# Eight shared PSUM banks and three PV blocks a unit in an attention and GLU kernel on one core

## The chip, the cores and the metric

One Trainium2 chip, one of its cores. The metric is the time of one execution on the device in microseconds (us); lower is better. The kernel before has a median of 1634.21 us over three executions (1633.94 to 1635.79).

## The reference, cut to what matters

The input x has 2048 rows of 512 numbers. The result mixes two branches by a gate for each row:

```
g = sigmoid((x * gate_w).sum(-1))
q = x @ wq          # 32 heads of 16 numbers
k = x @ wk; v = x @ wv      # one head, shared by all 32
p = softmax(q . k * 16 ** -0.5)
a = (p @ v, heads side by side) @ wo
h = (x @ w_gate) * (x @ w_up)       # 512 -> 1792
b = h @ w_down
out = g * a + (1 - g) * b
```

Nearly all of the work is in three places: the scores (32 heads of 2048 x 2048 with a depth of only 16), their exponentials, and the bilinear GLU branch.

## The kernel before, in words

The attention is cut into 64 units. A unit is a chunk of 512 rows of x (c), a group of eight heads (g) and a quarter of the chunk (t, 128 queries). For each unit three kinds of work stand on TensorE:

- **s1** (`p1`, matmul L690): the scores with the queries on the partitions, 32 matmuls of 512 columns. VectorE takes the largest score of each row out of the PSUM bank (L691). The negative maximum goes through DRAM back into two rows of the unit's Q tile.
- **s2** (`p2`, matmul L731): the scores again with the keys on the partitions, the maximum already taken off, 32 matmuls of 512 columns. ScalarE writes the exponentials from the bank into a tile P (L732).
- **PV** (`pv`, matmul L744): P times V. A round takes two key blocks: four matmuls in the program's order, on four column groups of 32, and eight in the trace, which shows each of these matmuls twice. A unit has eight rounds, all summed in one PSUM bank, the accumulator. After the last round ScalarE copies it out (L748), and a chain of DMAs and GpSimd operations (`o_chain`) brings it to the output projection.

Everything else of any size (the query projections, the GLU matmuls, the output projection) is cut into jobs of twelve products. Each product is run as two matmuls of 64 rows, one in each half of the array. They are the **filler** (`fill`, L854, tiles called ms). s1, s2 and filler matmuls use one half of the array's rows each, so that two run side by side; the kernel calls the halves lanes 0 and 1. PV uses all the rows.

TensorE's order is written out by hand. `ORDER` (L51) is a string of 144 letters that is run through once a unit: a and b are s1 on lane 0 and 1, c and d are s2, e and f filler, p a PV round. A run of p's without another letter between is called a **block** here, and what lies between two passes of the same letter a **cycle**; each other letter is a **slot**. Ahead of the first pass a loop runs s1 and filler alone until 25 s1 matmuls of each lane are done (`LEAD`).

A tile of PSUM fills one of eight banks, and a bank is named when the program is built. While it writes the order out, the Python code keeps a clock for each engine (`State`, L394): when each bank would come free, when TensorE could go on. `claim` (L417) gives an s1, s2 or filler matmul the bank that would be free soonest. The chip knows nothing of these clocks: there, a matmul that begins in a bank waits on a semaphore for the engine that read the bank's last tenant, wherever the planner's clock thought it was. Before the change seven banks (`NB = 7`) are in this pool, and bank 7 is the accumulator's alone (`pv`, L737 on).

The two lanes of a filler job sum into one bank. Where lane 1 would begin a job whose products of lane 0 are not yet known to be through, `fill` first calls `fence` (L811): two small transposes with a copy by VectorE between them, for which TensorE has to wait once.

The chunk of x that the filler works on changes three times. Those places are called turns in what follows; they fall into the 18th, the 33rd and the 48th unit's stretch or right behind.

Of the kernel before, what the change touches and what calls it, by code (L numbers as in the profile page):

```python
# [32 lines left out]
PBUF = 12  # L33
# [5 lines left out]
GAP = 50.0  # L39
# [2 lines left out]
EXP, EXP_END = 482.0, 604.0  # L42
COPY, COPY_END = 497.0, 597.0
PV_IN, PV_ROUND, PV_LAST, PV_END, PV_OUT = 331.0, 866.0, 438.0, 617.0, 647.0
NB = 7
LAT, LAT_LAST = 1.0, 0.5
LEADJOBS = 6
O0, O1 = 0, 0


ORDER = (  # L51
    "cbebedefcfefcbefedebefcfafedefadefcfebefefebededafefedafefedafcfefcbefef"
    "cfcfafadppdafcaffafcfcfefafefcbedebefedefafedebebedebappcdcbabppadcbabpp"
)
HALVES = (slice(0, 64), slice(64, 128))
KROWS = (slice(0, 48), slice(64, 112))
# [4 lines left out]
def mix_kernel(ctx: ExitStack, tc: tile.TileContext, x, wq, wk, wv, wo, wg, wu, wd, gw, out):  # L61
# [87 lines left out]
    def bank(i, name):  # L149
        return psum.tile([128, 512], F32, name=name, tag=f"bank{i}")  # L150
# [25 lines left out]
    st = {"gen": None, "next": None, "q": 0, "tail": False, "idle": False}  # L176
# [217 lines left out]
    class State:  # L394


        def __init__(self):
            self.nl, self.last, self.pd = [0.0, 0.0], -1e9, 0.0
            self.dve, self.act = 4000.0, 500.0
            self.free, self.wrote = [0.0] * NB, [0] * NB  # L400
            self.known, self.seq = 0, 0
            self.n1, self.n2, self.npv = [0, 0], [0, 0], 0
            self.ready, self.slot, self.acc = {}, [[0.0, 0.0] for _ in range(PBUF)], 0.0
            self.inpv = False

        def issue(self, l, wait):
# [10 lines left out]
        def claim(self):  # L417
            b = self.free.index(min(self.free))
            if st["idle"] or self.npv == 0:
                b = max((i for i in range(NB) if self.free[i] <= max(min(self.nl), self.free[b])), key=lambda i: self.wrote[i])  # L420
            self.known = max(self.known, self.wrote[b])
# [21 lines left out]
        def pv(self):  # L443
            s = self.npv
            at = self.last + PV_ROUND - PV_LAST if self.inpv else max(self.last + PV_IN, self.pd)
            for i in range(2):
                for v in range(2):
                    t, seq = self.ready.pop((s + i, v))
                    at, self.known = max(at, t), max(self.known, seq)
            if s % NJ == 0:  # L450
                at = max(at, self.acc)
            for i in range(2):
                self.slot[(s + i) % PBUF] = [at + PV_LAST + PV_END] * 2
            self.last = self.pd = at + PV_LAST
            self.inpv = True
            self.nl = [self.last + PV_OUT] * 2
            self.seq += 1
            self.npv += 2
            if self.npv % NJ == 0:
                self.act = max(self.act, self.last + PV_END) + COPY  # L460
                self.acc = self.act + COPY_END - COPY + GAP

    def evac(j, p, part):
        clock["act"] = max(clock["act"], clock["T"] + SEEN)
# [113 lines left out]
    def o_chain(c, g, t, osb):  # L578
        if (c, t) not in oT:
            oT[c, t] = work.tile([128, 4, 128], F32, name="oT", bufs=2)  # L580
        dst = oT[c, t][:, g]
        d = dram.tile([128, 512], F32, name="do", tag="do", bufs=4)
        dn = work.tile([128, 2, 8], F32, name="dn", bufs=2)
        raw = work.tile([128, 2, 128], F32, name="raw", bufs=2)
        rb = work.tile([128, 128], F32, name="rb", bufs=2)
        d4 = d.rearrange("(p a r) (s q) -> p a r s q", p=2, a=2, s=4)

        m = LAT if units.index((c, g, t)) < NU - 2 else LAT_LAST

        def store():  # L590
            nc.sync.dma_start(d, osb)
            later(5500.0 * m, load)

        def load():
            for par in range(2):
                nc.sync.dma_start(dn[:, par], d[par * 64 + 16:par * 64 + 64:32, :].rearrange("a (m e) -> a m e", e=8))
            for par in range(2):
                for half in range(2):
                    nc.sync.dma_start(raw[half * 64:half * 64 + 64, par],
                                      d4[par, half, 0:DH].rearrange("r s q -> s r q"))  # L600
            later(6000.0 * m, add)

        def add():
            den = work.tile([128, 8], F32, name="den", bufs=2)
            nc.gpsimd.tensor_tensor(den, dn[:, 0], dn[:, 1], op=OP.add)
            end = spend("pool", 200.0)
            nc.gpsimd.tensor_tensor(raw[:, 0], raw[:, 0], raw[:, 1], op=OP.add)
            spend("pool", 400.0)
            at(end + 2500.0 * m, lambda: recip(den))

        def recip(den):
            rc = work.tile([128, 8], F32, name="rc", bufs=2)
            nc.vector.reciprocal(rc, den)
            at(spend("dve", 150.0) + 250.0, lambda: rows(rc))

        def rows(rc):
            dr = dram.tile([8, 128], F32, name="dr", tag="dr", bufs=4)
            nc.sync.dma_start(dr.rearrange("h (m e) -> (h m) e", e=8), rc)
            later(3000.0 * m, lambda: spread(dr))

        def spread(dr):
            nc.sync.dma_start(rb, dr.rearrange("h (o q) -> h o q", o=1).to_broadcast([8, DH, 128]))
            later(3500.0 * m, norm)

        def norm():
            nc.gpsimd.tensor_tensor(dst, raw[:, 0], rb, op=OP.mult)  # L626
            spend("pool", 400.0)
            if (c, g, t) == units[NU - 2]:
                oh, ol = st["o"] = w512("oh", F32R, 2), w512("ol", F32R, 2)
                o = oT[c, t].rearrange("p g q -> p (g q)")[:, 0:384]  # L630
                done = split2(oh[:, 0:384], ol[:, 0:384], o) + 300.0
                st["p"] = bank(6, "wo")
                front.append(Job(
                    lambda: [m for k in range(3)
                             for m in mm3((oh[:, KS[k]], ol[:, KS[k]]), (woh[:, k], wol[:, k]))],
                    None, lambda: done if st["tail"] else 1e18, st["p"]))
            elif g == NG - 1:
                o = oT.pop((c, t)).rearrange("p g q -> p (g q)")
                oh, ol = w512("oh", F32R, 2), w512("ol", F32R, 2)
                done = split2(oh, ol, o) + 300.0  # L640
                front.append(Job(
                    lambda: [m for k in range(4)
                             for m in mm3((oh[:, KS[k]], ol[:, KS[k]]), (woh[:, k], wol[:, k]))],
                    lambda p, i: y_add(c, t, p, gg[:, c * NT + t:c * NT + t + 1]), lambda: done))
        at(E.acc + 50.0, store)
# [11 lines left out]

    def o_last(c, g, t, osb):
        def pick():
            p = bank(5, "pick")  # L660
            for v in (1, 0):
                for s in range(4):
                    nc.tensor.matmul(p[:, v * 128:v * 128 + 128], st["sel"][v][:, s], osb[:, KS[s]],  # L663
                                     start=(s == 0), stop=(s == 3))
            rb = work.tile([128, 128], F32, name="rb", bufs=2)
            nc.vector.reciprocal(rb, p[:, 128:256])
            o = oT[c, t][:, g]
            nc.vector.tensor_tensor(o, p[:, 0:128], rb, op=OP.mult)
            oh, ol = st["o"]
            split(oh[:, KS[3]], ol[:, KS[3]], o)  # L670
            front.append(Job(lambda: mm3((oh[:, KS[3]], ol[:, KS[3]]), (woh[:, 3], wol[:, 3])),
                             lambda p, i, at=clock["T"] + 2500.0: y_add(c, t, p, gg[:, c * NT + t:c * NT + t + 1]),
                             lambda at=clock["T"] + 2500.0: at, st["p"], False))
        later(900.0, pick)
# [59 lines left out]
    acc = {}  # L734

    def pv(s):
        u, j = divmod(s, NJ)  # L737
        if j == 0:
            acc[u] = bank(7, "acc")
        for i in range(2):  # L740
            src = P.pop(s + i)
            for half in range(2):
                b = 32 * (2 * i + half)
                nc.tensor.matmul(acc[u][b:b + 32, :], V[:, j + i], src[:, half], start=(j == 0), stop=(j == NJ - 2))  # L744
        if j == NJ - 2:
            def out():
                osb = w512("osb", F32, 2)
                nc.scalar.copy(osb, acc.pop(u))  # L748
                (o_last if u == NU - 1 else o_chain)(*units[u], osb)
            later(0.0, out)  # L750


    p = bank(6, "warm")
# [6 lines left out]
    p = ms_bank(1)  # L760
# [37 lines left out]
    st["gen"] = ffn_jobs()  # L798
    E = State()
    E.n1, E.dve, E.act = [done, done], 2000.0, 2000.0  # L800
    E.free = [2500.0, 3500.0, 0.0] + [1500.0] * (NB - 3)
    fetched = 2
    jobs = {}

# [140 lines left out]
    while events or front or st["gen"] or st["next"]:  # L945
        run_events()
        if peek():
# [3 lines left out]
            for part in range(j.parts):  # L951
                p = j.p
                if p is None:
                    p = ms_bank(turn)
# [24 lines left out]
```

## Time and profile before

| what | value |
| --- | --- |
| median of three executions | 1634.21 us |
| span of the profiled execution | 1631.8 us |
| what lies around the span, median less span | 2.4 us |
| granted TensorE clock | 1.000 |
| TensorE matmuls busy | 1622.0 us (99%) |
| VectorE busy | 1386.9 us (85%) |
| ScalarE busy | 1239.0 us (76%) |
| GpSimd busy | 719.4 us (44%) |

PE is TensorE, DVE is VectorE, ACT is ScalarE and POOL is GpSimd. Matmuls of the two lanes overlap and their ends are modelled, so that the 99% doesn't say that nothing is lost: what counts is when one matmul starts after the one before. A row of the timeline gives the start, the time from the start of the first to the end of the last, the engine, the line, out<-in, and how many instructions are merged (x16). In brackets stands the idle time ahead of it and who ended it. L12 is line 12 of the kernel.

### The profile page before, as it was taken

How to read it: one execution, taken by the hardware profiler on the slowest of the kernel's cores; microseconds unless marked ns; L12 is line 12 of the kernel's file. 1: busy time of each engine (PE TensorE's matmuls, PEld its weight loads, DVE VectorE, ACT ScalarE, POOL GpSimd, SP SyncE). 2: the span in 40 equal slices, each digit the busy share in tenths (PEclk: the TensorE clock that was granted, in tenths of full speed). 3: DMA queues.
4: the chain of work that ended last, by engine and by line, in shares of the span. 5: the costliest groups of instructions: out<-in, count | busy, mean ns of one | idle time of the engine just before them, and what ended most of it. 6: DMA issues, size and time to landing. Idle time of an engine off the chain costs nothing.

```text
span 1631.8 us, 35270 instructions
## 1 busy us (share of the span) xinstructions
PE 1622.0 (99%) x13126; PEld 1047.5 (64%) x13126; DVE 1386.9 (85%) x2415; ACT 1239.0 (76%) x2395; POOL 719.4 (44%) x855
## 2 busy tenths in 40 slices
PE   9999999999999999999999999999999999999999
PEld 7666666666675666666665666666665676676665
DVE  6988888888887888888887888888888888898871
ACT  4787777787786787787786777787787787787785
POOL 5515642724532652625422651643724641642621
PEclk9999999999999999999999999999999999999999
DMA  5463322212122221212122221222223221222101
GB/s 160 163 220 117 91 67 59 60 52 75 51 86 83 77 68 55 63 54 68 56 90 74 74 65 54 66 59 61 58 54 117 65 78 50 62 66 58 35 27 38
DMA packets 184991, 121.44 MB, mean 74 GB/s; under 512 B 46196, under 2 KB 154356, under 8 KB 184820
## 3 DMA queue, kind: packets, MB, share of 16 engines
q1 hardware_dynamic: 183620, 118.87, 24.3%
q8 instruction: 103, 1.69, 0.4%
q14 instruction: 68, 0.56, 0.1%
q10 hardware_dynamic: 1200, 0.33, 0.1%
HBM read 82.96 MB, written 36.17 MB: 73 GB/s over the span
## 4 chain that ended last, share of the span: by engine, by line
PE 96%; DVE 2%; issue 1%; DMA 1%; ACT 0%; POOL 0%; SPq 0%; POOLq 0%; ACTq 0%; DVEq 0%
PE ms L854 33%; PE acc L744 29%; PE s L731 18%; PE s L690 14%; DVE mx L691 2%; PE ms L142 1%; ACT P L732 0%; DMA dq<-oh 0%; PE warm L755 0%; PE wo L142 0%; DMA rb<-dr 0%; DMA dr<-rc 0%; SPq L218 0%; PE pick L663 0%; DMA Q<-dq 0%
## 5 line engine op out<-in xcount | busy, mean ns | idle before, releaser
L691 DVE TENSOR_REDUCE mx<-s 128x1 f32<-128x512 f32 x2048 | 1309.6, 684 | 180.4 <-PE s L690 103.3
L732 ACT ACTIVATE P<-s 128x512 f32<-128x512 f32 x2048 | 1079.1, 604 | 272.1 <-PE s L731 201.0
L731 PE MATMUL s<-Q,KK 50*128 50x512 f32 x2048 | 747.7, 412 | 0.3
L690 PE MATMUL s<-KK,Q 48*128 48x512 f32 x2048 | 691.6, 407 | 1.9 <-ACT P L732 1.0
L744 PE MATMUL acc<-P,V 128*32 128x512 f32 x4096 | 492.5, 598 | 0.0
L731 PEld LDWEIGHTS s<-Q,KK 50*128 50x128 f32 x2048 | 351.8, 185 | 188.1 <-issue 99.8
L690 PEld LDWEIGHTS s<-KK,Q 48*128 48x128 f32 x2048 | 338.7, 185 | 99.4 <-ACT P L732 55.4
L854 PE MATMUL ms<-xh,wh 64*128 64x512 f32 x920 | 338.9, 392 | 0.0
L854 PE MATMUL ms<-xl,wh 64*128 64x512 f32 x920 | 336.6, 391 | 0.0
L854 PE MATMUL ms<-xh,wl 64*128 64x512 f32 x920 | 321.4, 392 | 0.0
L744 PEld LDWEIGHTS acc<-P,V 128*32 128x32 f32 x4096 | 108.9, 109 | 234.8 <-issue 197.2
L527 POOL TENSOR_TENSOR hf<-gs 128x512 f32<-128x512 f32 x55 | 70.6, 1284 | 361.5 <-ACT gs L518 314.5
L356 POOL TENSOR_TENSOR y<-y,yt 128x512 f32<-128x512 f32 x63 | 81.0, 1286 | 234.3 <-ACT yt L355 223.9
L854 PEld LDWEIGHTS ms<-xh,wh 64*128 64x128 f32 x920 | 163.5, 185 | 9.9 <-DVE mx L691 0.4
L854 PEld LDWEIGHTS ms<-xl,wh 64*128 64x128 f32 x920 | 164.8, 186 | 7.7
L854 PE MATMUL ms<-wdh,hh 64*128 64x512 f32 x448 | 168.0, 394 | 0.1
L854 PE MATMUL ms<-wdl,hh 64*128 64x512 f32 x448 | 167.2, 393 | 0.6 <-POOL wdl L130 0.6
L854 PEld LDWEIGHTS ms<-xh,wl 64*128 64x128 f32 x920 | 157.2, 186 | 9.5 <-issue 0.3
L854 PE MATMUL ms<-wdh,hl 64*128 64x512 f32 x448 | 160.0, 393 | 0.0
L130 POOL TENSOR_TENSOR wl<-wn,wh 128x512 fp32r<-128x512 f32 x116 | 149.5, 1289 | 9.3
L626 POOL TENSOR_TENSOR oT<-raw,rb 128x128 f32<-128x128 f32 x63 | 29.1, 463 | 163.0 <-DMA rb<-dr 163.0
L748 ACT COPY osb<-acc 128x512 f32<-128x512 f32 x64 | 37.6, 587 | 78.6 <-PE acc L744 78.6
(154 smaller groups left out, 1331.3 us busy)
## 6 DMA issues: line engine op xcount, KB each, us to landing
do<-osb SPq DMA_DIRECT2D x63, 256.0 KB
wn<-in_B_w_gate_dram SPq DMA_DIRECT2D x56, 256.0 KB
wn<-in_B_w_up_dram SPq DMA_DIRECT2D x56, 256.0 KB
wdn<-in_B_w_down_dram SPq DMA_DIRECT2D x56, 256.0 KB
Q<-dq SPq DMA_DIRECT2D x384, 32.0 KB
raw<-do SPq DMA_DIRECT2D x252, 32.0 KB
dq<-oh SPq DMA_DIRECT2D x16, 256.0 KB
dq<-ol SPq DMA_DIRECT2D x16, 256.0 KB
```

Of the source, the lines that this page charges most:

```text
L130: nc.gpsimd.tensor_tensor(lo, src, hi.bitcast(F32), op=OP.subtract)
L142: nc.tensor.matmul(p, l, r, start=start and i == 0, stop=stop and i == len(prods) - 1)
L356: nc.gpsimd.tensor_tensor(y[c, t], y[c, t], tmp, op=OP.add)
L527: nc.gpsimd.tensor_tensor(hf, gu[0], gu[1], op=OP.mult)
L626: nc.gpsimd.tensor_tensor(dst, raw[:, 0], rb, op=OP.mult)
L690: nc.tensor.matmul(p, q[r, slot], KK[r, kq * 512:(kq + 1) * 512], start=True, stop=True)
L691: nc.vector.tensor_reduce(mx[u][:, half * 4 + slot, kq:kq + 1], p, axis=AX.X, op=OP.max)
L731: nc.tensor.matmul(p, KK[r, j * 128:(j + 1) * 128], q[r].rearrange("p s q -> p (s q)"), start=True, stop=True)
L732: nc.scalar.activation(P[s][:, half], p, AF.Exp, scale=0.25)
L744: nc.tensor.matmul(acc[u][b:b + 32, :], V[:, j + i], src[:, half], start=(j == 0), stop=(j == NJ - 2))
L748: nc.scalar.copy(osb, acc.pop(u))
L854: nc.tensor.matmul(j.p[part], lhs[HALVES[l]], rhs[HALVES[l]], start=(l == 0 and i == 0), stop=(l == 1 and end))
```

## The change

All eight banks are in the planner's pool (`NB = 8`). The accumulator has no bank of its own: at a unit's first round `pv` claims one, keeps it until the last round, and gives it back once ScalarE has copied it. `ORDER` is another string. It has the same letters (16 each of a, b, c and d, 36 each of e and f, eight p), but the eight rounds stand in three blocks (3, 2 and 3 rounds) and not in four (2, 2, 2, 2). Two banks that were named by number in the last steps (the last output projection, and the `pick` matmuls that sort out the last unit's result) give way if the accumulator holds them. The order of the instructions differs, and with it the banks; what is computed does not.

```
-NB = 7
+NB = 8
...
-    "cbebedefcfefcbefedebefcfafedefadefcfebefefebededafedafefedafcfefcbefef"
...
+    "adcbcfefefebedebedbedefcfebebcfefcfefafcfaefebededefbedebededefadeafeffc"
...
             if s % NJ == 0:
-                at = max(at, self.acc)
+                self.accb = self.claim()
+                at = max(at, self.free[self.accb])
+                self.free[self.accb] = 1e18
...
             if self.npv % NJ == 0:
                 self.act = max(self.act, self.last + PV_END) + COPY
-                self.acc = self.act + COPY_END - COPY + GAP
+                self.acc = self.free[self.accb] = self.act + COPY_END - COPY + GAP
+                self.wrote[self.accb] = self.seq
...
-                st["p"] = bank(6, "wo")
+                st["p"] = bank(5 + (E.accb == 5), "wo")
...
-            p = bank(5, "pick")
+            p = bank(3 + (E.accb == 3), "pick")
...
         if j == 0:
-            acc[u] = bank(7, "acc")
+            acc[u] = bank(E.accb, "acc")
...
-    E.free = [2500.0, 3500.0, 0.0] + [1500.0] * (NB - 3)
+    E.free = [2500.0, 3500.0, 0.0] + [1500.0] * (NB - 4) + [9000.0]
```

In the following rows of TensorE, s<-KK,Q is an s1 matmul, s<-Q,KK an s2 matmul, ms a filler matmul and acc a PV matmul (four make a round); what stands in brackets is the engine or the DMA queue whose semaphore the row waits for. First the 21st unit before the change, from the last slots ahead of its second block to the start of its fourth: the blocks have two rounds each.

```order
L690 MATMUL s_9024<-KK,Q 128x512 [waits DVE_49]
L690 MATMUL s_9027<-KK,Q 128x512 [waits Activation_49]
L744 MATMUL acc<-P,V 32x512 x8
L731 MATMUL s_9038<-Q,KK 128x512 [waits Activation_49]
L731 MATMUL s_9042<-Q,KK 128x512 [waits DVE_49]
L731 MATMUL s_9045<-Q,KK 128x512 [waits Activation_49]
L690 MATMUL s_9048<-KK,Q 128x512 [waits DVE_49]
L690 MATMUL s_9051<-KK,Q 128x512 [waits DVE_49]
L690 MATMUL s_9054<-KK,Q 128x512 [waits DVE_49]
L744 MATMUL acc<-P,V 32x512 x8
```

The same unit after the change, from the last slots ahead of its first block to its second one:

```order
L693 MATMUL s_8902<-KK,Q 128x512 [waits Activation_49]
L857 MATMUL ms_8734<-xh,wl 128x512
L857 MATMUL ms_8734<-xl,wh 128x512
L693 MATMUL s_8927<-KK,Q 128x512 [waits DVE_49]
L857 MATMUL ms_8804<-xh,wh 128x512
L734 MATMUL s_8931<-Q,KK 128x512 [waits Activation_49]
L747 MATMUL acc<-P,V 32x512 [waits DVE_49]
L747 MATMUL acc<-P,V 32x512 x11
L734 MATMUL s_8962<-Q,KK 128x512 [waits Activation_49]
L693 MATMUL s_8965<-KK,Q 128x512 [waits Activation_49]
L693 MATMUL s_8968<-KK,Q 128x512 [waits Activation_49]
L693 MATMUL s_8971<-KK,Q 128x512 [waits DVE_49]
```

A block of twelve rows (three rounds) stands where one of eight stood, and its first matmul now waits for VectorE: the accumulator's bank had an s1 tenant. In the whole program 192 blocks stand where there were 256, with as many slots and rounds. Last, the end of the program after the change, behind the last PV round:

```order
L857 MATMUL ms_25568<-wdl,hh 128x512
L818 MATMUL fence<-ident 32x32
L818 MATMUL fence<-ident 32x32 [waits DVE_49]
L857 MATMUL ms_25592<-wdh,hh 128x512
L857 MATMUL ms_25592<-wdh,hl 128x512
L857 MATMUL ms_25592<-wdl,hh 128x512
```

Before the change there is no fence anywhere in the program; now there is this one, with six filler matmuls behind it and then the `pick` matmuls.

More of the change, by code (lines that the diff above doesn't have):

```diff
@@ L51 @@
 ORDER = (
-    "cbebedefcfefcbefedebefcfafedefadefcfebefefebededafefedafefedafcfefcbefef"
-    "cfcfafadppdafcaffafcfcfefafefcbedebefedefafedebebedebappcdcbabppadcbabpp"
+    "adcbcfefefebedebedbedefcfebebcfefcfefafcfaefebededefbedebededefadeafeffc"
+    "afcfafafcfaffafcpppcbabcbppbcbedcfefefedaefadefedefadefcbefcfefafedabppp"
 )
@@ L402, in __init__ @@
             self.n1, self.n2, self.npv = [0, 0], [0, 0], 0
-            self.ready, self.slot, self.acc = {}, [[0.0, 0.0] for _ in range(PBUF)], 0.0
+            self.ready, self.slot, self.acc, self.accb = {}, [[0.0, 0.0] for _ in range(PBUF)], 0.0, 7
             self.inpv = False
```

## The prediction

> **What bounds the kernel now.** I read the page first: what is busy, and what the chain that ended last is made of.
>
> ```profile
> span 1631.8 us, 35270 instructions
> PE 1622.0 (99%) x13126; PEld 1047.5 (64%) x13126; DVE 1386.9 (85%) x2415; ACT 1239.0 (76%) x2395; POOL 719.4 (44%) x855
> PE 96%; DVE 2%; issue 1%; DMA 1%; ACT 0%; POOL 0%; SPq 0%; POOLq 0%; ACTq 0%; DVEq 0%
> ```
>
> 96% of the chain is TensorE, so the time is the length of TensorE's queue: the slots, the PV rounds, what is lost at the borders between them, and waits. Next I read the groups by line.
>
> ```profile
> L691 DVE TENSOR_REDUCE mx<-s 128x1 f32<-128x512 f32 x2048 | 1309.6, 684 | 180.4 <-PE s L690 103.3 <-PE s L731 45.4 <-PE ms L854 14.6
> L732 ACT ACTIVATE P<-s 128x512 f32<-128x512 f32 x2048 | 1079.1, 604 | 272.1 <-PE s L731 201.0 <-PE s L690 57.9 <-PE ms L854 0.8
> L744 PE MATMUL acc<-P,V 128*32 128x512 f32 x4096 | 492.5, 598 | 0.0
> ```
>
> VectorE and ScalarE are idle for 180 and 272 us, mostly waiting for TensorE. They are not the bound, but not far from it: a unit gives VectorE 32 reductions.
>
> Then the timeline of TensorE around one PV block, and two rows further on for the pace of the slots. The row of x8 comes from an answer that was cut to begin inside that block, behind the end of its first round; its start is that of the second round.
>
> ```profile
> 606.73 0.39 PE L690 MATMUL s<-KK,Q 48*128 48x512 f32 x1
> 606.73 0.40 PE L731 MATMUL s<-Q,KK 50*128 50x512 f32 x1
> 607.05 1.92 PE L744 MATMUL acc<-P,V 128*32 128x512 f32 x16
> 607.94 1.04 PE L744 MATMUL acc<-P,V 128*32 128x512 f32 x8
> 608.91 0.50 PE L731 MATMUL s<-Q,KK 50*128 50x512 f32 x1
> 609.25 0.39 PE L731 MATMUL s<-Q,KK 50*128 50x512 f32 x1
> ...
> 622.25 0.39 PE L731 MATMUL s<-Q,KK 50*128 50x512 f32 x1
> ...
> 625.97 0.39 PE L854 MATMUL ms<-xl,wh 64*128 64x512 f32 x1
> ```
>
> From 622.25 to 625.97 lie 16 steps of a pair of lanes: 0.2325 us a step, and one step takes two slots. A PV round takes 0.89 (607.05 to 607.94). The last pair ahead of the block starts at 606.73, the first behind it at 608.91, which is 2.18, and the next one follows after 0.34 in place of 0.23. So a block of two rounds lengthens the queue by 2.18 + 0.11 - 0.23 = 2.06, of which two rounds are 1.78. **A block as such costs 0.28.**
>
> With these prices a cycle can be summed and held against the trace. These rows are block starts, each cycle taken from a block to the same block of the next unit: one undisturbed cycle (740.46 to 764.54, with its second block at 759.04), the three that were not, and the first and the last unit's first blocks.
>
> ```profile
> 70.66 1.06 PE L744 MATMUL acc<-P,V 128*32 128x512 f32 x8
> 482.12 1.92 PE L744 MATMUL acc<-P,V 128*32 128x512 f32 x16
> 510.54 1.92 PE L744 MATMUL acc<-P,V 128*32 128x512 f32 x16
> 740.46 1.92 PE L744 MATMUL acc<-P,V 128*32 128x512 f32 x16
> 759.04 1.92 PE L744 MATMUL acc<-P,V 128*32 128x512 f32 x16
> 764.54 1.92 PE L744 MATMUL acc<-P,V 128*32 128x512 f32 x16
> 848.49 1.92 PE L744 MATMUL acc<-P,V 128*32 128x512 f32 x16
> 878.16 1.92 PE L744 MATMUL acc<-P,V 128*32 128x512 f32 x16
> 1229.27 1.92 PE L744 MATMUL acc<-P,V 128*32 128x512 f32 x16
> 1256.32 1.92 PE L744 MATMUL acc<-P,V 128*32 128x512 f32 x16
> 1605.19 1.92 PE L744 MATMUL acc<-P,V 128*32 128x512 f32 x16
> ```
>
> 136 slots are 68 steps, 15.81 us; four blocks of 2.06 are 8.24; together 24.05. The cycle from 740.46 to 764.54 took 24.08. So in an undisturbed cycle TensorE waits for next to nothing (0.03), and the order alone sets the pace. From 70.66 to 1605.19 lie 63 cycles with a mean of 24.36. Of the 17.6 us above 24.08, the three cycles of the turns hold 12.9: 28.42, 29.67 and 27.05 us long, 4.3, 5.6 and 3.0 too much. In the first of them TensorE waits for banks:
>
> ```profile
> 492.39 0.39 PE L690 MATMUL s<-KK,Q 48*128 48x512 f32 x1
> 493.00 0.50 PE L690 MATMUL s<-KK,Q 48*128 48x512 f32 x1 [0.23 <-ACT P L732]
> ```
>
> 0.61 between two matmuls in place of 0.23: a wait for one bank costs 0.38.
>
> **The change part by part. Fewer blocks.** The new cycle has the same 136 slots (15.81) and 8 rounds, but three blocks: two of three rounds (2.06 + 0.89 = 2.95 each) and one of two, 7.96 in all. That is 23.77, or 0.28 less; over 64 units 64 x 0.28 = **17.9 us less**. The trace shows no block of three rounds. If its third round took half of what lies between a block's start and the next matmul (1.86 / 2 = 0.93), a unit would gain 0.20 and the whole 12.8. If it took 0.88 (the 1.92 of x16 less the 1.04 of x8), the whole would gain 19.2. I take the start to start of 0.89, since that is measured from round to round.
>
> The Trainium skill, TensorEngine Tiling (Array Packing), Key Properties, says that a change of tiling mode, unlike a change of tile, drains TensorE. It gives no price; by it 128 of 512 changes go, and the gain hangs on the number of blocks, as it does above.
>
> **The accumulator's claim, and one more bank.** The first matmul of a unit's first block now waits for the reduction that last read its bank, and all that stands behind it on TensorE waits with it. In return an s1, s2 or filler matmul can have an eighth bank in the long stretch of 88 slots without PV. Whether waits appear is a matter of how far VectorE and ScalarE fall behind. VectorE's and ScalarE's rows of the undisturbed cycle:
>
> ```profile
> 742.88 8.36 DVE L691 TENSOR_REDUCE mx<-s 128x1 f32<-128x512 f32 x12 [0.31 <-PE s L690]
> 754.25 6.67 DVE L691 TENSOR_REDUCE mx<-s 128x1 f32<-128x512 f32 x11 [0.31 <-PE s L731]
> 761.69 1.89 DVE L691 TENSOR_REDUCE mx<-s 128x1 f32<-128x512 f32 x3 [0.67 <-PE s L690]
> 761.42 1.57 ACT L732 ACTIVATE P<-s 128x512 f32<-128x512 f32 x3 [1.87 <-PE s L731]
> ```
>
> Back to back a reduction takes (6.67 - 0.69) / 10 = 0.60 and an exponential (1.57 - 0.60) / 2 = 0.49. The eleven reductions from 754.25 on belong to the 44 slots between the unit's first and second block; they end at 760.92, 1.9 us behind the start of the second block at 759.04. So VectorE is three reductions late there, with seven banks in the pool, and the cycle still has no more than 0.03 of waits. In the new order the densest place is right ahead of the first block of three rounds: the last 25 slots hold seven a's, five c's and d's. That is 2.9 us of TensorE, 4.2 of VectorE and 2.5 of ScalarE beside filler copies. VectorE falls 1.3 us behind, less than the 1.9 that the old order bears, and the block of 2.95 behind it lets it catch up. Against this stands that ScalarE is nearly full in the same slots. In the built programs the shortest way from a bank's last matmul to the next claim in an undisturbed cycle is 11 slots (1.28 us) in both, and the middle one 14 slots in both. I take one wait of 0.38 in eight cycles, 0.05 a cycle, **3 us more** in all; none at the low end, and one in every second cycle at the other, 12 us.
>
> PV itself needs exponentials that are ready: in the new order the last half of a P tile for the third round of the second long block stands three slots ahead of that block, so that its round starts 0.35 + 0.32 + 1.78 = 2.4 us later. An exponential needs its matmul's 0.39, its own 0.60 and its turn on ScalarE; nothing is put down for it.
>
> **The turns.** At these three places the planner's bank choices are short of the chip's times. The same three turns are in the new program, at the same units, and claims within 10 slots (under 1.2 us) of a bank's last matmul number 66 in them, where it was 71. I leave them as they are, with a third of 12.9 either way: **0, from -4 to +4 us**.
>
> **Start and end.** Ahead of the first PV round the new order has 19 s1 matmuls in place of 14, and VectorE is busy without a gap there:
>
> ```profile
> 54.47 14.48 DVE L691 TENSOR_REDUCE mx<-s 128x1 f32<-128x512 f32 x23
> ```
>
> Five more reductions are 3.0 us of VectorE, eight more slots 0.9 of TensorE; 2.1 would be late if VectorE's idle time behind that row gave nothing back. I take half, **1 us more**; from 0 to 2. At the end the queue on TensorE runs without a gap from the last PV block into `pick`:
>
> ```profile
> 1618.05 1.92 PE L744 MATMUL acc<-P,V 128*32 128x512 f32 x16
> 1619.90 0.50 PE L854 MATMUL ms<-wdl,hh 64*128 64x512 f32 x1
> ...
> 1622.76 0.39 PE L854 MATMUL ms<-wdl,hh 64*128 64x512 f32 x1
> 1623.08 2.05 PE L663 MATMUL pick<-osb,wn 128*128 128x128 f32 x16
> ```
>
> The fence stands there now. It holds TensorE for a matmul, a short copy and a semaphore each way. The nearest rows are the bank wait of 0.38 and a reduction with the matmul ahead of it (0.39 + 0.69); I take **0.9 us more**, from 0.4 to 1.5.
>
> **The sum.** -17.9 + 3 + 0 + 1 + 0.9 = -13.0. Against the profiled execution that is a span of 1618.8. What lies around the span (2.4 us up to the median) stays, so from 1634.2 it is 1621.2.
>
> **The rivals.** *Bank waits eat most of the gain.* VectorE and ScalarE have the same work in a cycle that is shorter by 0.28, and 39 of the 64 reductions and exponentials now stand in one stretch of 88 slots. With one wait of 0.38 in every second cycle, 12 in place of 3, the time is 1630. For it speaks the bracket of ScalarE at 761.42: it idles through the PV blocks (1.87) and so must do its work between them, and longer blocks make that worse. Against it speaks the late burst of eleven. 0.15.
>
> *Slower: evacuation becomes the bound at the first long block.* If the accumulator's bank, claimed behind seven dense reductions, comes free late in every cycle, the block starts late in every cycle and everything with it. At 0.38 a cycle the price is 24.3: 1634.2 - 17.9 + 24.3 + 1.9 = 1642.5. It decides from 0.28 a cycle on. VectorE's 85% speaks for it; that its burst is 1.3 and not 1.9 late speaks against it. 0.05. The Trainium skill names this danger (the same page, PSUM Bottleneck): tiling makes TensorE faster, but not the emptying of PSUM, which may then be the bottleneck. The undisturbed cycle does not agree so far: TensorE there loses 0.03 of 24.08.
>
> *The turns grow.* More dense slots and the planner's wrong clock together could double the 12.9 there, which gives 1634. 0.06.
>
> *The gain isn't in the blocks.* If the 0.28 belongs to the rounds (each third round pays its own border), nothing is saved and the fence and the start remain: 1634.2 + 1.9 = 1636. The 607.94 row speaks against it, since the second round has no such border. 0.04.
>
> **How the numbers follow.** The forecast, 1621, has the remaining 0.70. Its own bounds give 1634.2 - 19.2 - 4 + 0.4 = 1611 at the best, and with the first rival at its upper end about 1630. I take 1612 to 1630. This holds the forecast and nearly all of the first rival, and leaves out the other three and a little at each end, not more than 0.2. A difference of 0.2% (3.3 us) is about what a measurement of this kernel can tell from none. Faster by more than that, below 1631: the 0.70, 0.12 of the first rival, 0.03 of the turns and a little of what misses by less, 0.87. Within 0.2%: 0.08. Slower: 0.05.
>
> **What would show it.** In the profile after, 192 blocks, those of three rounds 2.8 long (1.92 + 0.89); undisturbed cycles of 23.8, at most 23.9, from first block to first block; VectorE's share near 86%. Waits ahead of the first long block that name `mx` or `P` in brackets in most cycles would prove the first or second rival; cycles of 24.1 with no waits the last one. At the end, a gap of about 0.9 at the fence. The forecast is wrong if the mean undisturbed cycle is above 24.0, or if the three turns lose more than 17 us.

## The result, and the profile after

The changed kernel takes 1617.36 us (median of four executions, 1617.22 to 1619.62) against 1634.49 for the kernel before: a ratio of 0.990 with an interval of 0.9886 to 0.9914, 17.1 us less. One execution of the kernel with a block cut in two, further on, ran at a granted clock of 0.767 and took 1924.14 us; it is left out there. The profiled executions differ by 16.2 us:

```profile
span 1615.6 us, 35492 instructions
PE 1605.9 (99%) x13128; PEld 1002.7 (62%) x13128; DVE 1350.2 (84%) x2417; ACT 1204.5 (75%) x2395; POOL 719.3 (45%) x855
PE 89%; issue 1%; POOL 0%; DMA 0%; ACT 0%; SPq 0%; DVE 0%; POOLq 0%; DVEq 0%
```

TensorE is nearly the whole chain, as before (its share is 89% where it was 96%; the page's shares add up to 90% now, and it doesn't say what the rest is). These are TensorE's rows around the first two blocks of a unit of the changed kernel, and the first block of the next unit:

```profile
698.91 0.40 PE L734 MATMUL s<-Q,KK 50*128 50x512 f32 x1
699.24 2.78 PE L747 MATMUL acc<-P,V 128*32 128x512 f32 x24
701.95 0.49 PE L734 MATMUL s<-Q,KK 50*128 50x512 f32 x1
...
702.85 1.92 PE L747 MATMUL acc<-P,V 128*32 128x512 f32 x16
704.70 0.50 PE L693 MATMUL s<-KK,Q 48*128 48x512 f32 x1
...
723.21 2.78 PE L747 MATMUL acc<-P,V 128*32 128x512 f32 x24
```

A block of three rounds is 2.78 long, 0.86 more than one of two. It starts 0.33 behind the last matmul ahead of it, where the old blocks started after 0.32. Over all 64 units the medians are 0.34 and 0.32: the accumulator's new wait costs about 0.02 a unit, some 1 us in all. This cycle took 23.97; the median of the undisturbed ones is 23.93, and was 24.15 before.

The start, the turns and the end (the row of x12 is cut off by the end of that answer's window, so that only its start counts):

```profile
71.82 1.49 PE L747 MATMUL acc<-P,V 128*32 128x512 f32 x12
481.59 2.78 PE L747 MATMUL acc<-P,V 128*32 128x512 f32 x24
507.79 2.78 PE L747 MATMUL acc<-P,V 128*32 128x512 f32 x24
1204.12 2.78 PE L747 MATMUL acc<-P,V 128*32 128x512 f32 x24
1230.49 2.78 PE L747 MATMUL acc<-P,V 128*32 128x512 f32 x24
1256.28 2.78 PE L747 MATMUL acc<-P,V 128*32 128x512 f32 x24
1589.67 2.78 PE L747 MATMUL acc<-P,V 128*32 128x512 f32 x24
...
1604.42 0.39 PE L857 MATMUL ms<-wdl,hh 64*128 64x512 f32 x1
1604.73 0.20 PE L818 MATMUL fence<-ident 32*32 32x32 f32 x1
1605.20 0.20 PE L818 MATMUL fence<-ident 32*32 32x32 f32 x1 [0.27 <-DVE ft L819]
1605.33 0.50 PE L857 MATMUL ms<-wdh,hh 64*128 64x512 f32 x1
```

The first turn's cycle is 26.20 long, the third turn now stretches over two, of 26.37 and 25.79. So 16.2 us come together like this, from the starts of the first blocks of all 64 units in both traces (each part rounded):

| part | us |
| --- | --- |
| undisturbed cycles, 63 x (23.93 - 24.15) | -13.9 |
| the turns: 8.8 above the median cycle, where it was 12.6 | -3.8 |
| the first three cycles: 2.7 above it, where it was 1.1 | +1.7 |
| the first PV round: at 71.82, where it was at 70.66 | +1.2 |
| from the last unit's first block to the end (the fence's 0.7 in it) | -0.6 |
| small deviations of the other cycles | -0.7 |

### The profile page after: what moved, and what is told of

Its sections match the earlier page's. It is cut to its first block, busy times and chain, and to the rows that moved or that the text cites. A ratio compares the mean times of both kernels' runs of the same rounds, so it can differ in the third digit from the quotient of the medians.

```text
span 1615.6 us, 35492 instructions
## 1 busy us (share of the span) xinstructions
PE 1605.9 (99%) x13128; PEld 1002.7 (62%) x13128; DVE 1350.2 (84%) x2417; ACT 1204.5 (75%) x2395; POOL 719.3 (45%) x855
## 4 chain that ended last, share of the span: by engine, by line
PE 89%; issue 1%; POOL 0%; DMA 0%; ACT 0%; SPq 0%; DVE 0%; POOLq 0%; DVEq 0%
PE ms L857 32%; PE acc L747 27%; PE s L734 16%; PE s L693 14%; PE wo L142 0%; DMA raw<-do 0%; DMA do<-osb 0%; PE pick L666 0%; ACT P L735 0%; SPq L602 0%; POOL hf L530 0%; POOL wdl L130 0%; POOL hl L130 0%; SPq L599 0%; DVE y L348 0%
## 5 line engine op out<-in xcount | busy, mean ns | idle before, releaser
L694 DVE TENSOR_REDUCE mx<-s 128x1 f32<-128x512 f32 x2048 | 1275.0, 684 | 202.4 <-PE s L734 90.1
L735 ACT ACTIVATE P<-s 128x512 f32<-128x512 f32 x2048 | 1061.9, 649 | 252.5 <-PE s L693 150.6
L734 PE MATMUL s<-Q,KK 50*128 50x512 f32 x2048 | 758.8, 409 | 0.7 <-ACT P L735 0.2
L693 PE MATMUL s<-KK,Q 48*128 48x512 f32 x2048 | 713.5, 408 | 1.3 <-DMA Q<-dq 0.7
L747 PE MATMUL acc<-P,V 128*32 128x512 f32 x4096 | 479.2, 597 | 0.0
L857 PE MATMUL ms<-xh,wh 64*128 64x512 f32 x920 | 331.3, 394 | 0.0
L857 PE MATMUL ms<-xl,wh 64*128 64x512 f32 x920 | 315.5, 393 | 0.0
L857 PEld LDWEIGHTS ms<-xl,wh 64*128 64x128 f32 x920 | 157.6, 185 | 6.8
L857 PE MATMUL ms<-wdl,hh 64*128 64x512 f32 x448 | 160.6, 396 | 0.6 <-POOL wdl L130 0.6
L857 PEld LDWEIGHTS ms<-wdh,hh 64*128 64x128 f32 x448 | 81.4, 185 | 8.1 <-ACT osb L751 0.5
```

The source lines that it names most:

```text
L693: nc.tensor.matmul(p, q[r, slot], KK[r, kq * 512:(kq + 1) * 512], start=True, stop=True)
L694: nc.vector.tensor_reduce(mx[u][:, half * 4 + slot, kq:kq + 1], p, axis=AX.X, op=OP.max)
L734: nc.tensor.matmul(p, KK[r, j * 128:(j + 1) * 128], q[r].rearrange("p s q -> p (s q)"), start=True, stop=True)
L735: nc.scalar.activation(P[s][:, half], p, AF.Exp, scale=0.25)
L857: nc.tensor.matmul(j.p[part], lhs[HALVES[l]], rhs[HALVES[l]], start=(l == 0 and i == 0), stop=(l == 1 and end))
```

## Taking the change apart

Theory A in the expectations is the prediction's: what a unit saves is the borders of its blocks, and banks matter only where TensorE waits for them. Against it stand the rivals: the gain is in the bank, or in the rounds, not in the borders.

**The eight-bank pool alone.** The old order and the changed kernel's banks. Two letters of the order, four places apart, are exchanged, since otherwise a fence would come up in each unit.

```
-    "cbebedefcfefcbefedebefcfafedefadefcfebefefebededafefedafefedafcfefcbefef"
+    "cbebedefcfefcbefedebefcfafedefadefcfebefefebededadefefafefedafcfefcbefef"
-NB = 7
+NB = 8
...
```

> The old order with the eight-bank pool (one f and one d four letters apart are exchanged, so that no fence comes up; 256 blocks of two rounds). Theory A (the gain is the 64 blocks that go; the pool matters where banks run short): undisturbed cycles stay at 24.1, the three turns lose 6 to 9 us in place of 12.6, time 1627 to 1631. Rival B (the gain comes from the eighth bank): cycles well under 24.1, time 1617 to 1622.

Measured: 1629.49 us, ratio to the kernel before 0.9974 (0.9964 to 0.9984).

```profile
629.32 1.92 PE L747 MATMUL acc<-P,V 128*32 128x512 f32 x16
653.45 1.92 PE L747 MATMUL acc<-P,V 128*32 128x512 f32 x16
```

24.13 from unit to unit, as before the change; the turns lose 8.5 us where it was 12.6. This is theory A's cycle and time: where next to nothing waits for a bank, an eighth changes next to nothing.

**The new order alone.** Seven banks in the pool, bank 7 for the accumulator alone, as before the change. (The first line is the kernel's own; under "The change" the old order's first half lacks two of its 72 letters.)

```
-    "cbebedefcfefcbefedebefcfafedefadefcfebefefebededafefedafefedafcfefcbefef"
...
+    "adcbcfefefebedebedbedefcfebebcfefcfefafcfaefebededefbedebededefadeafeffc"
...
```

> The new order with seven banks in the pool and bank 7 for the accumulator alone (192 blocks). Theory A: the block price is saved as in the changed kernel, but waits for banks ahead of the first long block grow from 0.2 to 0.3 to 0.6 a cycle and the turns lose 15 us or more: 1625 to 1645. Rival B: without the eighth bank no gain is left, 1634 or more. If the order alone carries the gain and banks don't matter: 1617.

Measured: 1686.52 us, ratio 1.0322 (1.0306 to 1.0337): 53 us slower than before the change. That is far outside of theory A's 1625 to 1645; of the times expected, only the rival's open "1634 or more" holds it. The blocks are those of the changed kernel, but the cycle is 24.93:

```profile
652.67 2.78 PE L744 MATMUL acc<-P,V 128*32 128x512 f32 x24
677.60 2.78 PE L744 MATMUL acc<-P,V 128*32 128x512 f32 x24
```

The loss lies in one place. From the start of the second long block to the next unit's first block, the long stretch, are 14.31 us in place of the changed kernel's 13.29; the rest of the cycle is equal (10.61 and 10.60; medians). Here are rows of the weight loads' waits, by whom they waited for, of this kernel:

```profile
PEld s L731 <- ACT P L732: 31.0, 140, 0.7
PEld s L690 <- ACT P L732: 26.7, 133, 0.7
PEld s L690 <- DVE mx L691: 25.5, 112, 0.8
PEld s L731 <- DVE mx L691: 14.4, 66, 0.6
```

and of the changed kernel:

```profile
PEld s L693 <- ACT P L735: 38.9, 205, 0.7
PEld s L734 <- ACT P L735: 22.0, 102, 0.8
PEld acc L747 <- DVE mm L702: 13.3, 55, 0.2
PEld s L693 <- DVE mx L694: 2.5, 6, 0.8
```

The times in them also hold waits that hid behind running matmuls. But s1 and s2 matmuls wait for VectorE 178 times in the first kernel, and hardly ever in the second, where its one row of any size is the accumulator's claim: with one bank fewer in the long stretch both engines hold TensorE up. The pool alone gives -4 us and the order alone +53; together they give -17. The parts don't add, and neither theory holds by itself: the blocks save their price only with the eighth bank.

**The price of a block.** The changed kernel with its first long block cut in two, two slots apart:

```
-    "afcfafafcfaffafcpppcbabcbppbcbed..."
+    "afcfafafcfaffafcppcbpabcbppbcbed..."
```

> The changed kernel with its first block of three rounds split in two and one, two slots apart; letters and banks otherwise alike, 256 blocks. Theory A (a block as such costs 0.28 to 0.32 us): 64 x 0.3 = 18 to 20 us more than the changed kernel, 1635 to 1638. Rival (the border goes with the rounds, or is hidden by waits that stand there anyway): within 3 us of the changed kernel's 1617.

Measured: 1638.26 us, ratio to the kernel before 1.0029 (1.0017 to 1.0041): 20.9 us more than the changed kernel.

```profile
636.03 1.92 PE L747 MATMUL acc<-P,V 128*32 128x512 f32 x16
638.31 1.07 PE L747 MATMUL acc<-P,V 128*32 128x512 f32 x8
...
660.26 1.92 PE L747 MATMUL acc<-P,V 128*32 128x512 f32 x16
```

24.23 for this cycle and 24.25 for the median, 0.32 more than in the changed kernel; 20.9 / 64 = 0.33. A block as such has that price, and the rival that puts it down to the rounds is out. The difference stands where the edit is: from the first block to the block of two rounds that both kernels have are 3.95 us in place of 3.61, and the two other parts of the cycle are as long as they were (7.00 and 13.29 in both; medians), so that nothing hid it.

**Fewer blocks still.** The first two blocks joined:

```
-    "afcfafafcfaffafcpppcbabcbppbcbed..."
+    "afcfafafcfaffafcpppppcbabcbbcbed..."
```

> The changed kernel with its first two blocks joined to one of five rounds (the six slots between them stand behind it), 128 blocks. If the queue of TensorE alone sets the pace: 64 x 0.3 = 19 us less than the changed kernel, 1598. Theory A, with evacuation as the limit on it: ScalarE and VectorE idle through 4.5 us of PV and then owe more than the slots behind give, six claims a cycle come short by 3.7 us in sum, cycles of 24.0 to 24.6, 1620 to 1660.

Measured: 1696.27 us, ratio 1.0383 (1.0367 to 1.0398).

```profile
657.97 4.50 PE L747 MATMUL acc<-P,V 128*32 128x512 f32 x40
683.09 4.50 PE L747 MATMUL acc<-P,V 128*32 128x512 f32 x40
```

A cycle of 25.12, 1.2 longer with one block fewer. The direction is that of theory A, the size beyond it. The long stretch is as long as before (13.29); the loss lies right behind the five rounds, where 48 slots take 7.41 in place of 48 x 0.116 = 5.6. For ScalarE 4.5 us of PV are a hole:

```profile
662.99 1.08 ACT L735 ACTIVATE P<-s 128x512 f32<-128x512 f32 x2 [4.03 <-PE s L693]
```

A block saved is worth 0.33 only as long as ScalarE and VectorE get their work in time.

## Who holds the banks, and what the turns are

**Half the reduction, half the exponential.** Same order and banks as the changed kernel. In the first kernel each reduction leaves out half of its columns; in the second each exponential does, and PV reads the half that is made twice:

```
-        nc.vector.tensor_reduce(mx[u][:, half * 4 + slot, kq:kq + 1], p, axis=AX.X, op=OP.max)
+        nc.vector.tensor_reduce(mx[u][:, half * 4 + slot, kq:kq + 1], p[:, 0:256], axis=AX.X, op=OP.max)
```

> The changed kernel, same order and banks, but each s1 reduction reads only the first 256 of its 512 columns, so that VectorE has half the work there (the row maxima are then those of half of the keys). If VectorE holds the banks that TensorE waits for ahead of the first long block and at the turns: undisturbed cycles fall from 23.93 to 23.75, turns under 5 us in sum, 1600 to 1605. If it is ScalarE: cycles stay at 23.9, 1613 to 1618.

Measured: 1615.87 us, ratio 0.9891 (0.9877 to 0.9906); undisturbed cycles 23.90 in the median. A reduction takes 0.42 there in place of 0.68, and that gives 1.5 us.

```
-        nc.scalar.activation(P[s][:, half], p, AF.Exp, scale=0.25)
+        nc.scalar.activation(P[s][:, half, 0:256], p[:, 0:256], AF.Exp, scale=0.25)
...
-                nc.tensor.matmul(acc[u][b:b + 32, :], V[:, j + i], src[:, half], start=(j == 0), stop=(j == NJ - 2))
+                nc.tensor.matmul(acc[u][b:b + 32, :], V[:, j + i], src[:, half, 0:256].rearrange("p (o q) -> p o q", o=1).to_broadcast([128, 2, 256]), start=(j == 0), stop=(j == NJ - 2))
```

> The changed kernel, same order and banks, but each exponential makes only the first 256 of its 512 columns and PV reads those twice (the second half of each group of queries gets the first half's result). ScalarE's reading of a bank takes about half. If ScalarE holds the banks that TensorE waits for: undisturbed cycles fall from 23.93 to 23.75, 1600 to 1606. If it is VectorE: cycles stay at 23.9, 1613 to 1618.

Measured: 1603.98 us, ratio 0.9816 (0.9801 to 0.9831), 13.4 us less than the changed kernel.

```profile
621.58 2.78 PE L747 MATMUL acc<-P,V 128*32 128x512 f32 x24
645.34 2.78 PE L747 MATMUL acc<-P,V 128*32 128x512 f32 x24
```

23.76, and the median is 23.78: 0.15 a cycle less, 9.5 us over 63. Of that 0.13 comes from the long stretch (13.16 in place of 13.29; medians). It is ScalarE. What it holds is banks: PV's weight loads wait for exponentials only seven times in the changed kernel, 1.8 us in all. Its own timeline in the changed kernel, from the copy of the accumulator to the next unit's first block (at 723.21), shows why:

```profile
712.74 0.59 ACT L751 COPY osb<-acc 128x512 f32<-128x512 f32 x1 [1.84 <-PE acc L747]
713.23 5.01 ACT L735 ACTIVATE P<-s 128x512 f32<-128x512 f32 x10
718.10 0.71 ACT L355 ACTIVATE yt<-ms,gb 128x512 f32<-128x512 f32 x1
718.68 4.54 ACT L735 ACTIVATE P<-s 128x512 f32<-128x512 f32 x9
723.12 0.69 ACT L355 ACTIVATE yt<-ms,gb 128x512 f32<-128x512 f32 x1
```

Through the whole stretch of 88 slots it has no gap: nineteen exponentials and two copies back to back, behind 1.84 us of waiting for PV. (An exponential starts 0.48 after the one ahead, but a row can last 0.7: while the queue is full, rows begin before the one ahead has ended. The mean duration of L735 went from 604 to 649 ns without more work, while the copy of the accumulator, which follows an idle time, stayed at 587.) TensorE's steps right ahead of the first long block are stretched where ScalarE's release is late:

```profile
718.76 0.39 PE L857 MATMUL ms<-xl,wh 64*128 64x512 f32 x1
718.99 0.39 PE L857 MATMUL ms<-xh,wh 64*128 64x512 f32 x1
...
720.39 0.44 PE L857 MATMUL ms<-wdl,hh 64*128 64x512 f32 x1
720.67 0.39 PE L857 MATMUL ms<-wdh,hh 64*128 64x512 f32 x1
...
721.36 0.45 PE L857 MATMUL ms<-wdh,hh 64*128 64x512 f32 x1
721.65 0.39 PE L857 MATMUL ms<-wdh,hl 64*128 64x512 f32 x1
...
722.86 0.42 PE L734 MATMUL s<-Q,KK 50*128 50x512 f32 x1
```

From 718.76 to 722.86 lie 17 steps of a pair, 4.10 us, where 17 x 0.2325 = 3.95 would do. No single wait is long enough for a bracket in these rows; the steps are late by a few hundredths each.

**Can VectorE take copies off ScalarE?** Of each pair of GLU results in PSUM the first, or both, is copied by VectorE; the planner's clocks are told so (last line). The kernel for both has `if not st["idle"]:` there.

```
-            nc.scalar.copy(gu[i], p)
-            end = spend("act", COPY)
+            if i == 0 and not st["idle"]:
+                nc.vector.tensor_copy(gu[i], p)
+                end = spend("dve", RED)
+            else:
+                nc.scalar.copy(gu[i], p)
+                end = spend("act", COPY)
...
+                eng = "dve" if j.dve and not st["idle"] else "act"
```

> The changed kernel, but of each pair of GLU copies out of PSUM (gate and up, 56 pairs) the gate's is made by VectorE and not by ScalarE, and the planner's clocks know it. ScalarE is relieved of 56 x 0.49 = 27 us, VectorE burdened with 56 x 0.6 = 34. If ScalarE alone holds the banks: a part of the 10 us of waits goes, 1611 to 1615. If VectorE binds as soon as it has a little more: 1618 or more, with three claims a cycle that come 0.6 us short in the cycles that have such a copy.

Measured: 1621.60 us, ratio 0.9927 (0.9914 to 0.9941).

> As the one with half of the copies, but all 112 of them by VectorE: ScalarE less 55 us, VectorE more 67 us (its 84% becomes 88%). If ScalarE alone holds the banks: 1607 to 1613. If VectorE takes its place: above the one with half of the copies, 1618 to 1630.

Measured: 1637.01 us, ratio 1.0019 (1.0010 to 1.0027). Both are slower than the changed kernel's ratio of 0.990, the second by 20 us. Half of VectorE's reductions gives next to nothing, but a few more copies on it cost at once: the weight loads of s1 and s2 waited for VectorE for 3.9 us in sum, and now do for 19.0 and 43.1. The order leaves VectorE just enough, and ScalarE a little too little. Moving these copies from one to the other doesn't help. With other clocks the planner may also choose other banks; what share that has wasn't taken apart.

**The turns.** The last group of a chunk's down projection has two f tiles, and its jobs two parts of six products: a job then claims two banks, one a part, and each of its parts is copied out apart. Lane 1 runs a job behind lane 0, so that several of these banks are held at once. The groups were turned round, so that these jobs come first in a chunk:

```
-FGS = (range(0, 4), range(4, 8), range(8, 12), range(12, 14))
+FGS = (range(0, 2), range(2, 6), range(6, 10), range(10, 14))
```

> The changed kernel with the down jobs of a chunk grouped 2, 4, 4, 4 in place of 4, 4, 4, 2: the jobs of two parts, which hold a bank a part, stand at a chunk's beginning and not at its end. If these jobs make the turns' loss: the long cycles (18th, 33rd, 48th of the trace) go and come up two to four units behind each turn, and in the first chunk too. If the loss comes from x being loaded anew: they stay where they are. The time isn't the question here: at two turns 11 filler slots each stay empty, and go to the end; 1615 to 1625.

Measured: 1634.62 us, ratio 1.0004 (0.9995 to 1.0014).

```profile
436.45 2.78 PE L747 MATMUL acc<-P,V 128*32 128x512 f32 x24
462.63 2.78 PE L747 MATMUL acc<-P,V 128*32 128x512 f32 x24
486.55 2.78 PE L747 MATMUL acc<-P,V 128*32 128x512 f32 x24
510.53 2.78 PE L747 MATMUL acc<-P,V 128*32 128x512 f32 x24
```

The 18th cycle, which was 26.20, is 23.98 here (486.55 to 510.53), and the 33rd and 48th are as short. Long cycles stand two to four units behind each turn (the 20th and 21st, the 36th and 37th, the 51st and 52nd, 24.4 to 27.2) and in the first chunk (the 5th and 6th, 25.3 and 25.8). So the loss goes where the jobs of two parts go. Banks have a share in it, since an eighth one took about 4 us off the turns with either order. Whether the second copy has one too wasn't taken apart; with half an exponential, which relieves ScalarE and frees its banks sooner, the first two turns lose 1.6 each in place of 2.3 and 2.2. Two cycles were not foreseen: the 16th (436.45 to 462.63, 26.18) and the 32nd, in which filler slots stay empty and which are long all the same. Why is open. The time is worse than expected for them, and for 7.8 us of filler that is left for the end.

## Why the prediction was right

1621.2 us was predicted, within 1612 to 1630, and 1617.36 measured. The mechanism was the one named: fewer blocks, paid back in part by waits for banks. That the two together came so close is luck: -14.9 was predicted for them and -13.9 is what the undisturbed cycles gave, but one was 3 too small and the other about 4. By its steps:

- **Fewer blocks, -17.9 us.** The step "I take the start to start of 0.89" mis-sized it. The third round costs 0.86 (2.78 - 1.92), so that a block's own price is 2.06 - 2 x 0.86 = 0.34, and the block that was put back cost 20.9 / 64 = 0.33. The term is 21 us, above the upper end of 19.2 that was given for it. Blocks of one, two, three and five rounds (the kernels with a block cut in two and with two joined have the others) bear it out: from their start to the next matmul are 1.00, 1.85, 2.71 and 4.43, which is 0.86 a round.
- **Bank waits, +3, from 0 to 12.** Right in place, ahead of the first long block, but less than half of what came: 21 us of blocks less the 13.9 that the cycles gained leave about 7 us of new waits. Halving the exponentials takes out 9.5, more than the new ones: the "0.03" of waits in the kernel before was read from one cycle of 24.08, and the median of all 63 is 24.15, which makes it 0.10. The step that failed is the weighing: the late burst of eleven reductions showed that VectorE has room, and that was taken for both engines. ScalarE "nearly full in the same slots" was seen and set aside. Counting ScalarE's work in the long stretch would have shown it: behind 1.84 us of waiting for PV come a copy of the accumulator, nineteen exponentials and a filler's copy, which take 10.4 us without a gap (712.74 to 723.12); 88 slots of 0.116 are 10.2, or 10.4 with what the borders add at both ends, so that ScalarE has nothing to spare. The claim itself costs 0.02 a unit. No wait of PV for exponentials was put down, and hardly any came (1.8 us).
- **The turns, 0, from -4 to +4.** They lost 3.8 us less. That is the eighth bank: with the old order it took 4.1 off them too, and the new order with seven banks loses 12.6 there as before. The two errors, waits too small and turns not shortened, are of opposite sign.
- **The start, +1, at most 2.** The first PV round is 1.2 late; that half of VectorE's 2.1 would show was a choice, and it held. But the first three cycles lose another 1.7, which was in no term; why is open.
- **The fence, +0.9.** From 1604.42 to 1605.33 are 0.91 in place of 0.23: 0.7.
- **The rivals.** "Bank waits eat most of the gain" put them at 12 us; they are about 7, a third of the gain. The turns shrank instead of growing. "The gain isn't in the blocks" fell by the block that was put back. "Evacuation becomes the bound" did not come about here, but it is what decides: with seven banks the same order is 53 us slower than the old one, and with one more block joined 62. Its price had been put at 24 us.
- **The signs.** The undisturbed cycles were to be 23.8, at most 23.9, and are 23.93, under the 24.0 that would have spoken against the forecast. VectorE's share was to be near 86% and is 84%: the same 2048 reductions, 684 ns each in both traces, fill 1275.0 us in place of 1309.6, since more of them overlap.

What the prediction did not see is how far the new order depends on the pool. It took the pool for a small help beside the order; by the runs the order would have been a loss without it.

## What to carry to other kernels

A border between two kinds of matmul has a price that one pair of timeline rows gives, and putting one back is a clean test of it. But merging stretches of one kind makes the other engines idle and then owe: count, for each engine that empties PSUM, its work in the long stretch against that stretch's length, and take the fullest one, not the one whose rows look worst. Two edits that share a resource (a bank, an order) can be a loss and a trifle apart and a gain together, so time each alone before saying which one made the gain.

## What the runs showed that was not expected

A third round lengthens a PV block by 0.86, less than the 0.89 from the first round's start to the second's. In this case a queue that is always full shows in the rows' durations: exponentials went from 604 to 649 ns in the mean while their spacing stayed 0.48 to 0.49.
